# A new order for the instruction list of a convolution followed by a two-layer SiLU network

## The chip, the cores and the metric

The kernel runs on one core of one Trainium2 chip. The core has a matrix engine (TensorE, PE in the profile), a vector engine (VectorE, DVE), a scalar engine (ScalarE, ACT), GpSimd (POOL) and SyncE (SP). Each takes its instructions in the order in which the program gave them, and they wait for one another by semaphores. Matrix products go to eight accumulation banks, from which only VectorE and ScalarE read. Transfers are issued by SyncE or GpSimd. The metric is the device time of one execution in microseconds; lower is better.

## The reference

The input x has 8 sequences of 4096 tokens with 192 channels. A depthwise convolution over the last seven tokens comes first, its weights a softmax over the seven taps for each of eight heads of 24 channels. Its output, 32768 tokens by 192, goes through a network with 2048 hidden units.

```python
x_unf = x_pad[:, idx, :].reshape(B, S, K, H, group)
out = np.einsum('hk,bskhg->bshg', w, x_unf)      # conv, K = 7
...
h = x @ w_in                                     # 192 -> 2048
g = h * (1.0 / (1.0 + np.exp(-h)))               # SiLU
return (g @ w_out).astype(np.float32)            # 2048 -> 192
```

All is float32 on the chip.

## The kernel before, in words

**Blocks.** The tokens are cut into 32 blocks of 1024, two tiles of 512 each. Blocks 0 to 2 are started up by an own order (START); from then on one list (PLAN) is gone through once per pass, b = 3 to 33. Both are strings of tokens; `step` (from L863) turns a token into instructions. A leading "-" means the block before b, "=" two before, "+" the next block. The instructions are pinned: each engine gets them exactly in the order of the tokens. So one string sets the order on all engines at once, and a token that waits on an engine holds up that engine's later tokens. A token is carried out once per block; what was done already is skipped.

**What a pass does.** It makes the hidden values of block b, the output of block b - 1 and the convolved input of block b + 1.

**The conv (GpSimd, ScalarE, SyncE).** `ld.k` loads a third of the input (12 transfers of 64 KB for all), `i.k` turns it (VectorE), `ha.0` fetches the six tokens ahead of the block. `v.ki` is tap i of third k: ScalarE scales the shifted input into one of ten tiles `u` (L499) and GpSimd issues a transfer that adds this tile into `nat` (L500); the six adds of a third go into the same tile, one behind another. `sp.k` (SyncE, L521) copies the finished third to both halves of the 128 rows, into the tile `dup`, and `w.0` to `w.5` (VectorE) make sums and differences of it in the tile `win`.

**The products of h (L630).** Fast matrix multiplication, in 15 products for each of five groups g: `Pr.g` is a matmul with 64 rows and 128 columns over 512 tokens. Each product lies on one half of the rows: r = 0, 1, 2, 4, 5, 6, 11, 14 on the one (only P14.4 is an exception), the others on the other half; two products of different halves run side by side. The groups come in the order 0, 4, 1, 2, 3. The products of a group run in three chains, each chain in one bank, and between two products of a chain another engine reads the running sum:

- P5, copy u5, P2, copy u4, P6, copy u2, P1, copy u0, P0, copy u1, P14, S3. The copies are ScalarE's (L679), into the same ten tiles as the conv's; S is the SiLU (ScalarE, L691).
- P3, sum X2, P9, X4, P7, a5, P4, a1, P8, a0. The sums are VectorE's (L673); each takes one of the copies (X2 takes u2, X4 takes u4 and so on) and gives its tile back.
- P12, b1, P10, b5, and P13 and P11 into two more banks (after X2 and X4).

`L.nk` (L647) are the matmuls of one chunk that is multiplied plainly, three of them with 512 columns and three with two halves of 256.

**The output (L746).** `Di.je` is one slot of the second layer: four matmuls of 128 rows by 32 columns side by side over 512 tokens (128 tokens for i = 5), for j = 0 to 3 and e = 0, 1: 48 slots for a block. They read SiLU values and the differences `t.jk` of them, which VectorE makes (L714) in three rotating tiles. `y`, `x`, `z` (ScalarE, L804 to L812) and `M` (VectorE) gather the output from the banks, `o.i` turns it and `st.i` stores it (SyncE, L843, three transfers each).

**Where things stand.** In PLAN the output of block b - 1 comes first, all 48 D without a break, and then the products of block b. The one exception is at the list's head: P5.0 of block b and P8.3 of block b - 1, one on each half, directly behind the products of the pass before.

```python
nc.tensor.matmul(to[:, cols], raw(g, *LEFT[e][r], e), rhs[:, cols], start=first, ...)   # P
...
for q in range(4):
    nc.tensor.matmul(accs[b][at][SQ * q : SQ * q + SQ, to], lhs[...], rhs[...], ...)    # D
...
z = free.pop(0)                                                       # v: one of ten tiles
pin(nc.scalar.activation(z, src, AF.Copy, scale=tap))
pin(nc.gpsimd.dma_start(out=dst, in_=z, accum_op=ALU.add))
free.append(z)
```

Of the kernel before, what the change touches and what calls it, by code (L numbers as in the profile page):

```python
# [17 lines left out]
def kernel(  # L18
# [62 lines left out]
    PLAN = (  # L81
# [24 lines left out]
    )  # L106
    START = (
# [731 lines left out]
    def store_out(b, i):  # L839
        for q in range((HD if b else P) // SQ):  # L840
# [5 lines left out]
                )  # L846
            )

    plan = [slot.split() for slot in PLAN.split("|")]
    did, later = set(), []  # L850
    closing = f"S3.{QUEUE[-1]}"
    BACK = {"-": 1, "=": 2, "+": -1}
# [263 lines left out]
```

## Time and profile before

| what | value |
|---|---|
| runs | 2363.18, 2363.6, 2364.36 us (median 2363.6) |
| span of the profiled execution, first to last instruction | 2358.8 us |
| busy: PE, DVE, ACT, POOL | 2350.1, 1784.5, 1488.6, 531.0 us |
| transfers: packets' share of the 16 engines | 33.7% (GpSimd's queue), 23.1% (SyncE's) |
| mean granted clock of TensorE | 0.999 |

The profiled execution is reported by its span; the runs' times also hold what lies before the first and after the last instruction, 4.8 us at the median. A matmul is recorded as two parts (float32), 512 columns at some 0.59 us, and the parts overlap: the start of the next part tells more than a duration. Each row of a timeline has the start, the time from the first start to the last end, the engine and line, what is written and read, and a count; in brackets the idle time of the engine before it and what ended it. Rows with "128*32" are the output's D, rows with "64*128" the products. PEld is the loading of weights.

### The profile page before, as it was taken

The numbers are of one execution on the slowest core, as the hardware profiler recorded it, in microseconds if no ns is written. First come the engines' busy times: TensorE is split into PE (matmuls) and PEld (weight loads), VectorE is DVE, ScalarE is ACT, GpSimd is POOL, SyncE is SP. The second block draws the span as 40 slices with busy tenths as digits, with TensorE's granted clock in tenths as the row PEclk, the third lists the DMA queues.
The fourth block names the chain that finished last, engine by engine and source line by source line (L and its number), as shares of the span: only waits on it lengthen the run. The fifth ranks groups of instructions, "written<-read, shape, count | busy, mean of one in ns | idle before, by whom it ended". The sixth has DMA issues, their size and how long they took to land.

```text
span 2358.8 us, 45531 instructions
## 1 busy us (share of the span) xinstructions
PE 2350.1 (100%) x17630; PEld 1053.1 (45%) x17630; DVE 1784.5 (76%) x2373; ACT 1488.6 (63%) x2779; POOL 531.0 (23%) x672
## 2 busy tenths in 40 slices
PE   9999999999999999999999999999999999999998
PEld 4344444444444444444444454444444444444445
DVE  8898767787777787777877777767778777787676
ACT  5346766667656677566676666765667756667643
POOL 4911122211222112222112221122211222211200
PEclk9999999999999999999999999999999999999999
DMA  7234667656566655666556656556655566565511
GB/s 158 51 66 72 107 106 125 105 103 107 98 121 107 106 105 95 119 116 106 106 106 109 119 99 109 105 99 122 107 106 101 101 116 116 106 109 98 96 23 25
DMA packets 523833, 238.81 MB, mean 101 GB/s; under 512 B 431648, under 2 KB 436768, under 8 KB 523616
## 3 DMA queue, kind: packets, MB, share of 16 engines
q0 software_dynamic: 73024, 133.73, 33.7%
q1 hardware_dynamic: 447392, 101.78, 23.1%
q8 instruction: 138, 2.26, 0.4%
q10 hardware_dynamic: 3200, 0.39, 0.1%
q14 instruction: 79, 0.65, 0.1%
HBM read 31.46 MB, written 25.17 MB: 24 GB/s over the span
## 4 chain that ended last, share of the span: by engine, by line
PE 98%; DVE 1%; DMA 0%; ACT 0%; SPq 0%; issue 0%; ACTq 0%
PE ps L746 47%; PE ps L630 42%; PE ps L647 5%; PE ps L767 2%; PE ps L576 2%; PE ps L1015 1%; DVE t L714 0%; DMA dup<-nat 0%; PE ps L423 0%; ACT g L691 0%; DMA nat<-u 0%; SPq L843 0%; DVE g L673 0%; DVE cmb L163 0%; ACT u L163 0%
## 5 line engine op out<-in xcount | busy, mean ns | idle before, releaser
L500 POOL DMA_DIRECT2D nat<-u x504 | 431.9, 957 | 1598.0 <-ACT u L499 643.4
L630 PE MATMUL ps<-win,wr 64*128 64x512 f32 x1550 | 721.5, 598 | 0.0
L746 PE MATMUL ps<-g,wo 128*32 128x512 f32 x2976 | 703.0, 593 | 0.0
L630 PE MATMUL ps<-win,ws 64*128 64x512 f32 x1550 | 638.3, 599 | 0.9 <-ACT u L679 0.9
L746 PE MATMUL ps<-t,wo 128*32 128x512 f32 (+2 forms) x4528 | 547.8, 446 | 0.0
L679 ACT COPY u<-ps 128x512 f32<-128x512 f32 x775 | 442.5, 587 | 136.7 <-PE ps L630 88.6
L746 PE MATMUL ps<-t,wx 128*32 128x512 f32 x2976 | 495.6, 592 | 0.6 <-DVE t L714 0.5
L630 PE MATMUL ps<-dup,wr 64*128 64x512 f32 x868 | 424.1, 597 | 0.0
L691 ACT ACTIVATE g<-g 128x512 f32<-128x512 f32 x465 | 286.2, 633 | 175.5 <-DVE g L673 175.5
L714 DVE TENSOR_TENSOR t<-g,t 128x1024 f32<-128x1024 f32 x248 | 302.0, 1218 | 109.7 <-PE ps L746 107.4
L714 DVE TENSOR_TENSOR t<-g 128x1024 f32<-128x1024 f32 x248 | 302.5, 1220 | 103.9 <-PE ps L746 82.7
L809 ACT COPY yx<-ps 32x512 f32<-32x512 f32 x150 | 86.8, 579 | 421.5 <-PE ps L746 419.4
L673 DVE TENSOR_TENSOR g<-u,ps 128x512 f32<-128x512 f32 x465 | 314.2, 681 | 42.8 <-PE ps L630 32.0
L499 ACT ACTIVATE u<-xt,taps 128x512 f32<-128x512 f32 x504 | 340.0, 717 | 1.1
L630 PEld LDWEIGHTS ps<-win,wr 64*128 64x128 f32 x1550 | 272.1, 186 | 139.5 <-issue 75.6
L630 PE MATMUL ps<-dup,ws 64*128 64x512 f32 x682 | 328.2, 598 | 0.0
L630 PEld LDWEIGHTS ps<-win,ws 64*128 64x128 f32 x1550 | 255.8, 186 | 135.3 <-issue 58.6
L746 PEld LDWEIGHTS ps<-t,wo 128*32 128x32 f32 x4528 | 188.5, 110 | 273.3 <-issue 266.0
L691 ACT ACTIVATE g<-ps 128x512 f32<-128x512 f32 x465 | 267.8, 599 | 36.2 <-PE ps L630 33.6
L673 DVE TENSOR_TENSOR ps<-u,ps 128x512 f32<-128x512 f32 x310 | 215.0, 694 | 64.3 <-PE ps L630 26.7
L746 PE MATMUL ps<-g,wx 128*32 128x512 f32 x1488 | 250.5, 592 | 0.0
L824 DVE TENSOR_TENSOR cmb<-cmb,ps 96x512 f32<-96x512 f32 x150 | 102.2, 681 | 181.7 <-ACT yx L809 180.7
(92 smaller groups left out, 2010.5 us busy)
## 6 DMA issues: line engine op xcount, KB each, us to landing
nat<-u POOLq DMA_DIRECT2D x504, 256.0 KB, 4.0
dup<-nat SPq DMA_DIRECT2D x345, 128.0 KB, 3.0
nat<-in_x_dram SPq DMA_DIRECT2D x382, 64.0 KB, 2.7
out_dram<-osb SPq DMA_DIRECT2D x376, 64.0 KB, 2.0
raw<-in_moe_w_out_dram SPq DMA_DIRECT2D x8, 384.0 KB, 3.5
raw<-in_moe_w_in_dram SPq DMA_DIRECT2D x12, 192.0 KB, 4.4
ws<-wr POOLq DMA_DIRECT2D x8, 192.0 KB, 5.0
raw<-in_moe_w_in_dram SPq DMA_DIRECT2D x6, 128.0 KB, 3.0
```

What stands on the lines that cost most here:

```text
L499: pin(nc.scalar.activation(z, src, AF.Copy, scale=tap))
L500: pin(nc.gpsimd.dma_start(out=dst, in_=z, accum_op=ALU.add))
L576: nc.tensor.matmul(hs[a, n, e], rows(wr[j], e)[:, a, k, :], rows(d, e)[:, n, k, :], start=k == 0, stop=k == NK - 1,)
L630: nc.tensor.matmul(to[:, cols], raw(g, *LEFT[e][r], e), rhs[:, cols], start=first, stop=True, skip_group_check=True,)
L647: nc.tensor.matmul(banks[PLAIN_BANKS[n and 1 + e]][:, cols], rows(wr[j] if own == e else ws[j], e)[:, a, k, :], rows(dups[b], e)[:, SLOT[e ...
L673: pin(nc.vector.tensor_tensor(out_, u, v, op=op))
L679: pin(nc.scalar.copy(us[b, g, o][:, cols], t1[:, cols]))
L691: pin(nc.scalar.activation(h, src, AF.Silu))
L714: pin(nc.vector.tensor_tensor(t[i // 2][:, i % 2, :], u, v, op=ALU.subtract))
L746: nc.tensor.matmul(accs[b][at][SQ * q : SQ * q + SQ, to], lhs[:, e, SQ * k : SQ * k + SQ], rhs[:, e, ts(q, TB // 4) if i == 5 else to], st ...
L809: pin(nc.scalar.copy(to, acc[3 * (name[0] == "x") + k][n:P, :]))
L824: pin(nc.vector.tensor_tensor(out_, u, v, op=ALU.add))
```

## The change

PLAN is written anew, as one sequence of tokens in place of slots with bars (a slot had no other meaning than its tokens in order). It holds the same 300 steps. What differs:

- **P5.0 and -P8.3** stand no longer at the head of the list but in the middle of the output, with 22 D ahead of them in the list and 24 behind.
- **D0.21 and D1.20** lose their "-": they stand at the list's end, directly behind the block's last product, and so are the first D of the output.
- **a1.3, S5.2 and S5.4** get a "-": they move from the products to the head of the next pass.
- **sp.1** moves from the products to the output stage of the next pass; **ha.0, v.10 and v.20** likewise; **o.2 and st.2** move the other way, from two blocks back to one.
- The order of the other D, of the products, and of what the other engines do among them is new. The conv's steps v.25, v.26, v.06, v.15 and v.16 now stand among the products, in this order; before, these were v.16, v.04, v.05, v.06 and the next block's v.20 and v.10. Near the end of the products two of one half and then two of the other follow each other (P12.3, P8.2, then P11.3, P14.3); elsewhere the halves alternate by pairs.
- START gets "-o.2 -st.2 D0.21 D1.20" at its end, and is else the same.

The functions behind the tokens are unchanged. All lines behind the strings move up by five.

```diff
     PLAN = (
-        "+ld.1 P5.0 | -P8.3 -S1.4 -a0.2 -S4.3 | -D0.00 -t.01 -S0.2 | -D1.00 -S1.2 =o.2 v.00 "
-        "| -D2.01 -t.03 -S5.1 =st.2 | -D2.00 -b5.3 | -D1.20 -sp.0 v.21 -S5.3 | -D4.01 u5.0 "
...
-        "u2.1 b1.4 S4.4 | P5.2 | P10.4 X2.1 | P1.1 a1.4 u5.2 | P9.1 b5.4 | P2.2 u0.1 | P8.4 "
-        "X4.1 | P5.3 u4.2 | P7.1 a0.4 | P0.1 +i.1 u5.3 sp.1 | P12.1 a5.1 | P6.2 u1.1 | P3.2 "
...
-        "| P9.3 a5.2 S0.4 | P0.3 -st.0 | P10.2 S1.0 X4.3 | P14.2 u1.3 | P7.3 b5.2 +v.20 "
-        "-st.3 | P4.2 S0.1 | P12.3 a5.3 S3.1 | P14.3 +v.10 a1.2 | P13.3 | P4.3 S5.2 b1.3 | "
-        "P8.2 S2.3 | P11.3 a1.3 S3.3 | P10.3 S5.4 t.00 S3.2"
+        "-S4.3 -D1.11 -sp.0 -S1.4 -D0.11 -S5.1 -D1.01 -D0.01 -a0.2 -D1.00 -D0.10 -t.01 -t.03 "
+        "-D4.01 -D4.00 ha.0 v.10 -t.10 -t.11 -S5.4 -b5.3 -D2.00 v.20 v.21 -S0.2 -t.02 -D3.01 "
+        "-D2.11 -a1.3 -sp.1 -D0.31 -D2.01 -D2.10 v.00 -D3.00 -t.13 -t.12 -D5.01 v.11 v.22 -S1.3 "
+        "-D4.11 -D4.10 -D5.11 -D5.00 -S5.2 -S1.2 v.01 v.02 -D3.10 -D3.11 -S5.3 -t.20 v.23 v.24 "
+        "P5.0 -P8.3 v.12 -D1.30 -t.21 -D2.20 -t.23 -D4.21 -D4.20 -D5.10 -D2.21 -D0.20 -sp.2 "
+        "v.03 v.04 -D5.20 -t.22 -a0.3 -D3.21 -D1.10 -w.0 -S0.3 -t.30 -t.31 -t.32 v.13 -D2.31 "
+        "-D1.31 -t.33 -D5.30 -D0.00 v.05 -w.1 -w.2 -w.3 -w.4 -w.5 -D0.30 -D1.21 -D5.31 -D5.21 "
+        "-x2.1 v.14 -y1.0 -D4.30 -x2.0 u5.0 -D2.30 -y2.0 -z1.0 -D3.20 -M1.0 -D4.31 -x1.0 -x2.3 "
+        "-x2.2 -y0.0 +ld.1 -M2.0 -D3.31 -D3.30 -M3.0 -M4.0 P2.0 +ld.0 u4.0 P3.0 L.02 P5.4 u5.4 "
+        "-x0.0 L.00 P6.0 L.12 -M5.0 u2.0 L.01 X2.0 -M7.0 P2.4 u4.4 SL.0 L.10 L.11 P9.0 SL.1 "
+        "X4.0 SL.2 P1.0 u0.0 P6.4 u2.4 -M6.0 P13.0 S2.0 P5.1 u5.1 -o.3 P3.4 P7.0 P0.0 u1.0 "
+        "+ld.2 P12.0 P11.0 P1.4 X2.4 P9.4 a5.0 P4.0 P13.4 b1.0 v.25 S4.0 X4.4 P10.0 a1.0 b5.0 "
+        "P2.1 u0.4 P0.4 P7.4 -o.1 S2.4 a5.4 P11.4 v.26 P8.0 a0.0 u4.1 u1.4 S1.0 S4.4 P12.4 P6.1 "
+        "b1.4 u2.1 P14.4 P14.0 S3.4 P3.1 X2.1 P4.4 S3.0 a1.4 P5.2 u5.2 P10.4 b5.4 P9.1 P1.1 "
+        "X4.1 u0.1 -o.2 P2.2 v.06 P8.4 a0.4 P5.3 u4.2 P7.1 -st.3 a5.1 P0.1 -o.0 u5.3 u1.1 S5.0 "
...
+        "-st.2 a5.2 P4.2 P13.3 X4.3 P0.3 u1.3 b5.2 a1.2 P7.3 P12.3 S0.1 S0.0 a5.3 b1.3 P8.2 "
+        "+i.1 P11.3 P14.3 S2.3 S3.3 P4.3 P10.3 D0.21 D1.20 t.00 S0.4 -st.0 +i.0"
     )
     START = (
...
-        "P13.3 -o.3 P4.3 S3.2 b1.3 -st.3 +v.10 P8.2 +v.20 a1.3 P10.3 P11.3 S5.2 t.00 S2.3"
+        "P8.2 +v.20 a1.3 P10.3 P11.3 S5.2 t.00 S2.3 -o.2 -st.2 D0.21 D1.20"
     )
...
-    plan = [slot.split() for slot in PLAN.split("|")]
+    plan = [PLAN.split()]
```

99 rows, old and new, of tables (PLAN, START) are left out of this document.

## The prediction

> **What bounds the kernel now.** I read the page first, then the chain of waits in order of time, then short stretches of the timeline of TensorE, ScalarE and GpSimd.
>
> ```profile
> span 2358.8 us, 45531 instructions
> PE 2350.1 (100%) x17630; PEld 1053.1 (45%) x17630; DVE 1784.5 (76%) x2373; ACT 1488.6 (63%) x2779; POOL 531.0 (23%) x672
> 357.48 36.22 PE ps L746 x384
> 398.62 31.22 PE ps L630 x139
> 429.85 36.22 PE ps L746 x384
> ...
> 2243.82 36.22 PE ps L746 x384
> ```
>
> TensorE is never free, so the time is the length of TensorE's own queue. The last four rows are from the chain: one pass of the list is an output stage (L746) and a product stage (L647, L630). From the first to the last of these output stages lie 26 passes, (2243.82 - 357.48) / 26 = 72.55 us each. The first two are 429.85 - 357.48 = 72.37 apart, the usual pass; a few are longer. The median of the runs, 2363.6, is 4.8 above this span; I sum against the span and add 4.8.
>
> "Busy" hides the loss, so I set the necessary work beside it. All rows from here on are from timelines.
>
> ```profile
> 1011.34 0.60 PE L746 MATMUL ps<-g,wx 128*32 128x512 f32 x3
> 1012.20 0.61 PE L746 MATMUL ps<-t,wx 128*32 128x512 f32 x3
> 1053.39 0.59 PE L630 MATMUL ps<-win,ws 64*128 64x512 f32 x1
> 1054.25 0.59 PE L630 MATMUL ps<-win,wr 64*128 64x512 f32 x1
> 1051.08 0.38 PE L647 MATMUL ps<-dup,ws 64*128 64x256 f32 x1
> 1051.30 0.38 PE L647 MATMUL ps<-dup,wr 64*128 64x256 f32 x1
> 1051.57 1.13 PE L630 MATMUL ps<-win,ws 64*128 64x512 f32 x4
> ```
>
> A D token (four matmuls side by side, two parts each) takes 0.86; a pair of products, one on each half of the rows, also 0.86, one part 0.43. A 256-column part takes half, 0.215. A pass has 40 D at 0.86, 8 short D (D5) at 0.215, 39 pairs and 3 short pairs: 36.05 + 34.76 = 70.81. So 72.55 - 70.81 = 1.74 us per pass are lost, all in the product stage and at its two ends.
>
> **Changing between the two kinds of work.** The start order holds the thing that the change adds: D2.11, then P8.3 and P2.0, then D0.31.
>
> ```profile
> 157.53 0.60 PE L746 MATMUL ps<-t,wx 128*32 128x512 f32 x3
> 158.07 1.13 PE L630 MATMUL ps<-win,wr 64*128 64x512 f32 x4
> 159.13 1.06 PE L746 MATMUL ps<-g,wo 128*32 128x512 f32 x8
> 160.01 1.04 PE L746 MATMUL ps<-t,wo 128*32 128x512 f32 x8
> ```
>
> 157.53 is the second part of D2.11, 160.01 the D after next: 2.48 us for 0.43 + 0.86 + 0.86 = 2.15 of work. A pair in the middle of the output costs 0.33 to 0.34 beyond its own 0.86. In the kernel before, P5.0 and P8.3 stand at the end of the products and pay no change of their own. The changed list makes two more changes in each of 30 passes: 30 x 0.34 = **+10.1 us**. Nothing covers this, since both halves stop.
> The Trainium skill, "TensorEngine Tiling (Array Packing)", section Tiling Modes, says that changing the tiling mode drains TensorE, which speaks against this edit; the row above agrees, at 0.34 for both ways. Were there no drain, the sum below would come out 10.1 lower.
>
> **Short waits in the product stage.** The products accumulate in shared banks: a copy or a sum must have read the bank before the next product writes it.
>
> ```profile
> 1060.27 0.59 PE L630 MATMUL ps<-dup,wr 64*128 64x512 f32 x1
> 1060.28 0.69 PE L630 MATMUL ps<-dup,ws 64*128 64x512 f32 x1
> 1061.98 1.14 PE L630 MATMUL ps<-win,wr 64*128 64x512 f32 x4
> 1063.11 0.69 PE L630 MATMUL ps<-dup,ws 64*128 64x512 f32 x1
> 1063.64 0.59 PE L630 MATMUL ps<-dup,ws 64*128 64x512 f32 x1
> 1062.37 0.69 DVE L673 TENSOR_TENSOR u<-u,ps 128x512 f32<-128x512 f32 x1 [1.18 <-ACT g L691]
> 1064.04 0.58 ACT L679 COPY u<-ps 128x512 f32<-128x512 f32 x1 [0.24 <-PE ps L630]
> 1077.48 0.69 PE L630 MATMUL ps<-win,wr 64*128 64x512 f32 x1
> 1078.02 0.59 PE L630 MATMUL ps<-win,wr 64*128 64x512 f32 x1
> ```
>
> A matmul of 0.69 instead of 0.59 started late: its weights had waited too. 1063.11 is P10.4, which waits for b1.4 (the DVE row), which waits for P12.4, one pair earlier: it starts 0.15 late (the last part of the group before it at 1062.53, plus 0.43) and its second part comes after 0.53 instead of 0.43; together 0.25. P7.3 behind X4.3 (1077.48, 1078.02) has the same form and I price it the same. Behind a copy (0.58) instead of a sum (0.69) it is P14.4 at 1060.28, 0.02 + 0.10 = 0.12. With two pairs between, such a product is hardly ever late. P9.0 needs P6.0, copy u2.0 and sum X2.0 in a row: 1051.57 against 1051.30 + 0.215, plus 1.13 instead of 1.02, is 0.17.
>
> I counted these in both lists. Dependents with one pair between fall from 11 (eight behind a sum, three behind a copy) to 8 (four and four). Gone: P12.4/P10.4 0.25, P9.3/P7.3 0.25, P0.4/P14.4 0.12, and P9.0 0.17 (half a pair more between): 0.79. New on the half that ends last: P12.3/P10.3 0.25. Then P8.1 and P8.2: their sums a1 also have one pair; today they are covered because the half that P4 runs on is ahead. In the new list it is less ahead, so I charge one of them at 0.20. P6.0, P5.2 and P14.3 are new waits on the other half at 0.12 each, hidden as long as it stays ahead. Net -0.79 + 0.45 = **-0.34 per pass, -10 us**. Bounds: nothing saved if the other half becomes the last (0), or all that is now lost beside the changes, 1.74 less the 0.34 of the two changes that a pass has already, -1.4.
>
> **The transfers behind the copies.**
>
> ```profile
> 1058.64 0.84 POOL L500 DMA_DIRECT2D nat<-u  x1 [5.41 <-ACT u L499]
> 1063.19 0.85 POOL L500 DMA_DIRECT2D nat<-u  x1 [3.58 <-ACT g L691]
> 1066.58 1.07 ACT L679 COPY u<-ps 128x512 f32<-128x512 f32 x2 [1.10 <-DMA nat<-u]
> nat<-u POOLq DMA_DIRECT2D x504, 256.0 KB, 4.0
>   DMA nat<-u: 28.3, 24
> L499 ACT ACTIVATE u<-xt,taps 128x512 f32<-128x512 f32 x504 | 340.0, 717 | 1.1
> ```
>
> The last three are from the page's DMA issues, from the copies' line (24 waits, 28.3 us) and from the page's groups. A u copy takes one of ten tiles in turn, and a conv step (v) holds its tile until its transfer lands, 4.0 us after issue. Copy u4.2 takes the tile of v.06, seven pairs earlier, and v.06's transfer is issued late (1063.19) because v.05 adds into the same tile and goes first (1058.64). ScalarE stands 1.10, then P6.2 is late; this explains most of the 72.55 - 72.37 = 0.18. In the new list v.05 stands in the output stage, far from v.06; the nearest copies are u2.1 behind v.25 and u4.2 behind v.26. v.25 can run behind u1.0, which is ready some six pairs (5.5 us) ahead of u2.1, against 0.72 + 4.0 + a little; v.26 behind S2.4, some nine pairs ahead of u4.2, with v.25's landing in between. I take **-0.18 per pass, -5.4 us**; bounds 0 (the wait moves to u2.1) and the whole 28.3.
>
> **Edits that I cost at nothing, with their cover.** D0.21 and D1.20 move to the list's end, ahead of the other D: same count, and S3.2, which D1.20 reads, stands eight pairs earlier. a1.3, S5.2 and S5.4 move from the product to the output stage; there VectorE and ScalarE have room:
>
> ```profile
> 1010.40:1046.60 36.20, 36.20 (x385) 12.04 (x384) 23.97 (x26) 17.01 (x31) 11.15 (x13) 1.00 0.70 126
> 1046.60:1082.80 36.20, 36.20 (x172) 20.13 (x168) 30.11 (x47) 30.89 (x59) 4.37 (x6) 1.00 0.52 90
> L714 DVE TENSOR_TENSOR t<-g,t 128x1024 f32<-128x1024 f32 x248 | 302.0, 1218 | 109.7 <-PE ps L746 107.4
> dup<-nat SPq DMA_DIRECT2D x345, 128.0 KB, 3.0
> ```
>
> (columns: stretch, length, busy PE, PEld, DVE, ACT, POOL, clock, DMA; output stage, then products). P8.3 in the middle makes a0.3, S0.3 and t.30 to t.33 later. D5.30, ten D and two short D (9 us) behind P8.3, waits for t.33; behind P8.3 VectorE owes a0.3, w.0 and four t at 1.22 (L714's mean in the row above), with 0.69 (the DVE row above) for each of the others 6.3 us, plus what t.21 to t.22 leave over: by my count about 0.3 us remain, the tightest place. If that cover is gone, each 0.1 costs 3 us. The step sp.1 (four transfers, 3.0 us to landing) moves from the products to the output stage, some 9 us ahead of P5.0, which reads them; ha.0 and sp.0 stand ahead of it on SyncE, and behind them the loads. If it lands late, P5.0 stops all of TensorE in mid output. o.2 and st.2 move from the next pass's output to the products: one transpose on VectorE and three stores on SyncE. The start order only gains these tokens at its end.
>
> **Sum.** 10.1 - 10.2 - 5.4 = -5.5: 2358.8 - 5.5 = 2353.3 in the profile, **2358 us** in the runs.
>
> **Rivals.**
> (1) *The change of mode decides* (slower). The short waits are now partly hidden behind one another, two halves being late in turn; if taking four away only uncovers others, the 10.1 stands alone, or with the transfers' -5.4 half won: 2363.6 + 10.1 - 2.7 = 2371. It decides as soon as stage and transfers give back less than 0.34 per pass. For it: both halves lose about the same now. Against: the late rows that I can name (0.25, 0.25, 0.12, 0.17) all follow a dependency that the new list loosens. 0.27.
> (2) *A new wait in the output stage*, at D5.30 or P5.0, 0.3 per pass: +9, 2367. Against: 26 output stages in the chain are 36.22 long almost without exception, so the present order of the same steps runs without any. 0.14.
> (3) *Most of the lateness goes*: with fewer sums and copies in the product stage only 0.5 of the 1.4 remains besides the changes, -0.9 + 0.34 per pass: about 2347. 0.11.
> (4) *Misplaced halves.* Late in the new list stand P12.3, P8.2 (same half), then P11.3, P14.3 (other half). If matmuls start strictly in the order of the list, one pair's time is lost in 29 passes, 25 us: 2383. The trace speaks against it:
>
> ```profile
> 128.97 1.55 PE L630 MATMUL ps<-win,ws 64*128 64x512 f32 x5
> 130.02 1.02 PE L630 MATMUL ps<-win,wr 64*128 64x512 f32 x2
> ```
>
> The five are P0.2, P9.2 and P1.3; the two are P12.2, which the start order lists before P1.3. P1.3 (last part by 129.93) went first. 0.04. "TensorE: Matmul & The Clock Gate" in the Trainium skill (Part 3, The mechanism) says that matmuls start in strict order without reordering; the trace's 129.93 before 130.02 differs, so I keep the small chance.
>
> **Chances.** The sum holds 0.44, from about 2353 to 2364. A measurement of this kernel can tell 0.2%, 4.7 us. Faster by more: most of the forecast's part and (3), 0.44; within: the rest of the forecast's and the mild ends of (1) and (2), 0.26; slower: 0.30. Eight in ten reach from (3) to just past (1): 2346 to 2375. The forecast's own range is 2352 to 2364.
>
> **What would show it.** The chain's pieces: output stages broken in two by a short L630 piece, together 37.4 (36.22 + 0.86 + 0.34) long; product stages shorter by 0.86 + about 0.5; the pass 72.55 less 0.19. The copies' wait for nat<-u well below 28.3 us. No 0.69 rows at P10.4 and P7.3, one at P10.3. Wrong would be: a gap ahead of D5.30 or P5.0, P14.3 starting 0.86 after its turn, or product stages as long as now.

## The result, and the profile after

The changed kernel takes **2353.2 us** (median of 4 runs, 2352.7 to 2353.8). The kernel before, run beside it, takes 2363.9 (4 runs, 2363.2 to 2364.4). The ratio is 0.9955, with a 95% interval of 0.9941 to 0.9969: faster by 0.45%. The forecast was 2358; its own range was 2352 to 2364, and eight chances in ten lay from 2346 to 2375.

The page of the changed kernel, and its chain of waits in order of time (start, length, what, number of instructions). All line numbers are five lower than before: L741 is the output (D), L625 and L642 are products.

```profile
span 2351.0 us, 45656 instructions
PE 2343.4 (100%) x17630; PEld 1123.6 (48%) x17630; DVE 1802.6 (77%) x2373; ACT 1507.6 (64%) x2779; POOL 528.7 (22%) x672
```

```profile
230.14 1.06 PE ps L625 x4
231.20 17.54 PE ps L741 x192
...
283.56 18.82 PE ps L741 x192
302.38 1.06 PE ps L625 x4
303.44 17.54 PE ps L741 x192
...
2254.83 17.54 PE ps L741 x192
```

The output stage is now broken in two by a short piece of products, 18.82 + 1.06 + 17.54 = 37.42 long; 37.4 was forecast. The pass is 303.44 - 231.20 = 72.24, and over all 28 passes (2254.83 - 231.20) / 28 = 72.27. Before, the usual pass was 72.37 and the mean 72.55. So two things moved: the usual pass became 0.13 shorter, and the passes became equal. An excess of 0.18 per pass over the usual one went down to 0.03.

The profile fell by 7.8 and the runs by 10.7. The profiled execution of the changed kernel took 2352.7 in all, 1.7 more than its span. With the same 1.7, the profiled execution of before took about 2360.5 (an estimate), less than the median of its runs: the 4.8 that the prediction added was 1.7 outside the span and 3.1 because that one execution was a quick one. Executions of before lie between 2359.0 and 2365.8 in all the runs beside the experiments, those of the changed kernel within 1.1 us. So the irregular part of the passes is probably larger in the median run than in the profile that I predicted from; no second profile of before shows it.

The timeline of TensorE in the changed kernel, around the new pair, at D5.30, and at two places among the products of a later pass:

```profile
1022.39 2.75 PE L741 MATMUL ps<-t,wo 128*32 128x512 f32 x33
1025.06 0.69 PE L625 MATMUL ps<-dup,wr 64*128 64x512 f32 x1
...
1025.60 0.59 PE L625 MATMUL ps<-dup,wr 64*128 64x512 f32 x1
...
1026.12 0.63 PE L741 MATMUL ps<-g,wx 128*32 128x512 f32 x3
...
1026.58 0.60 PE L741 MATMUL ps<-g,wx 128*32 128x512 f32 x3
...
1035.17 0.40 PE L741 MATMUL ps<-t,wo 128*32 128x128 f32 x8
...
1207.07 0.59 PE L625 MATMUL ps<-win,ws 64*128 64x512 f32 x1
...
1207.59 0.69 PE L625 MATMUL ps<-win,wr 64*128 64x512 f32 x1
...
1219.95 0.59 PE L625 MATMUL ps<-win,ws 64*128 64x512 f32 x1
...
1220.58 0.69 PE L625 MATMUL ps<-dup,wr 64*128 64x512 f32 x1
...
1221.86 0.59 PE L625 MATMUL ps<-win,wr 64*128 64x512 f32 x1
...
1222.44 0.69 PE L625 MATMUL ps<-dup,ws 64*128 64x512 f32 x1
...
1222.97 0.59 PE L625 MATMUL ps<-dup,ws 64*128 64x512 f32 x1
```

The last part of the D before the pair starts at 1024.54 (the 2.75 from 1022.39 end at 1025.14, less 0.60 for one part) and is worth 0.43. P5.0 starts 0.09 after these 0.43 are over (1025.06), its second part is 0.11 late (1025.60), the next D 0.09 (1026.12) and its second part 0.03: 0.32 for the change both ways, and no wait for the transfers of sp.1. D5.30 (1035.17) starts without a gap. The two rows at 1207 are the product ahead of P7.1 and P7.1 itself, which starts 0.09 after its half is free (1207.07 + 0.43) and takes 0.69. The last rows are P11.3 (1220.58, on a half that was free at 1219.95 + 0.43, so 0.20 late) and P10.3 (1222.44 after 1221.86 + 0.43, 0.15 late, second part another 0.10). How near it was at D5.30 is in VectorE's timeline:

```profile
1033.66 1.22 DVE L709 TENSOR_TENSOR t<-g,t 128x1024 f32<-128x1024 f32 x1
```

This row is t.33. It ends at 1034.88, 0.29 ahead of D5.30.

The copies' line, and then the conv steps' line, idle time of ScalarE until a transfer and how often:

```profile
  DMA nat<-u: 0.3, 1
```

```profile
  DMA nat<-u: 2.9, 11
```

The copies waited 0.3 us in all for a transfer (before: 28.3), the conv steps 2.9.

In the product stage the usual pass now has these late places on the half that ends last, from the timeline of an even pass (late start plus late second part): P10.4 0.10, P9.1 0.06 + 0.10, P7.1 0.09 + 0.10, P10.3 0.15 + 0.10. Together 0.70. That is what is left of the pass above the necessary 70.81 and two times 0.34 for the changes of mode: 72.24 - 70.81 - 0.68 = 0.75. The same sum for the kernel before is 72.37 - 70.81 - 0.34 = 1.22; read in the same way, its late places on that half are P9.0 0.17, P14.4 0.12, P10.4 0.25, P9.1 0.10, P7.1 0.26 and P7.3 0.26, together 1.16.

So of 10.7 us: the changes of mode cost 10; the short waits gave back 0.47 x 30 = 14; the rest, some 7, I put down to the irregular part (0.15 x 30 = 4.5 of it are in the profiles; that most of the 3.1 above belongs to it too is argued, not shown). The experiments ask each of these.

### The profile page after: what moved, and what is told of

It reads as the page before. It is cut to its first block, busy times and chain, and to the rows that moved or that the text cites. A ratio compares the mean times of both kernels' runs of the same rounds, so it can differ in the third digit from the quotient of the medians.

```text
span 2351.0 us, 45656 instructions
## 1 busy us (share of the span) xinstructions
PE 2343.4 (100%) x17630; PEld 1123.6 (48%) x17630; DVE 1802.6 (77%) x2373; ACT 1507.6 (64%) x2779; POOL 528.7 (22%) x672
## 4 chain that ended last, share of the span: by engine, by line
PE 100%; DVE 0%; ACT 0%; issue 0%; ACTq 0%; DVEq 0%
PE ps L741 48%; PE ps L625 44%; PE ps L642 3%; PE ps L762 2%; PE ps L571 2%; PE ps L1010 1%; PE ps L418 0%; DVE cmb L158 0%; ACT u L158 0%; DVE osb L158 0%; DVE xt L460 0%; PE ps L444 0%; ACTq L944 0%; DVE zeros L158 0%; DVE xt L158 0%
## 5 line engine op out<-in xcount | busy, mean ns | idle before, releaser
L625 PE MATMUL ps<-win,wr 64*128 64x512 f32 x1550 | 685.8, 598 | 0.0
L741 PE MATMUL ps<-g,wo 128*32 128x512 f32 x2976 | 681.4, 594 | 0.0
L625 PE MATMUL ps<-win,ws 64*128 64x512 f32 x1550 | 629.5, 596 | 0.0
L674 ACT COPY u<-ps 128x512 f32<-128x512 f32 x775 | 452.3, 584 | 133.3 <-PE ps L625 110.7
L741 PE MATMUL ps<-t,wo 128*32 128x512 f32 (+2 forms) x4528 | 523.6, 446 | 0.0
L741 PE MATMUL ps<-t,wx 128*32 128x512 f32 x2976 | 474.7, 592 | 0.0
L686 ACT ACTIVATE g<-g 128x512 f32<-128x512 f32 x465 | 277.2, 625 | 262.6 <-DVE g L668 262.6
L625 PE MATMUL ps<-dup,wr 64*128 64x512 f32 x868 | 420.2, 598 | 0.0
L625 PEld LDWEIGHTS ps<-win,wr 64*128 64x128 f32 x1550 | 261.6, 187 | 113.4 <-issue 61.8
L625 PEld LDWEIGHTS ps<-win,ws 64*128 64x128 f32 x1550 | 254.6, 187 | 124.2 <-issue 53.5
L625 PE MATMUL ps<-dup,ws 64*128 64x512 f32 x682 | 291.9, 599 | 0.0
L741 PEld LDWEIGHTS ps<-t,wo 128*32 128x32 f32 x4528 | 180.3, 110 | 221.6 <-issue 192.7
L741 PE MATMUL ps<-g,wx 128*32 128x512 f32 x1488 | 251.4, 594 | 0.0
L741 PEld LDWEIGHTS ps<-t,wx 128*32 128x32 f32 x2976 | 121.2, 110 | 241.0 <-issue 240.6
L741 PEld LDWEIGHTS ps<-g,wo 128*32 128x32 f32 x2976 | 167.6, 110 | 135.3 <-issue 125.9
```

What stands on the lines that cost most here:

```text
L674: pin(nc.scalar.copy(us[b, g, o][:, cols], t1[:, cols]))
L686: pin(nc.scalar.activation(h, src, AF.Silu))
```

## Experiments

The theory at the start: the pass is the sum that the prediction made (mode changes up, short waits and transfers down). The rivals: the mode change costs more or less than 0.34, the short waits only cover one another, and the regular passes come from something else than the copies' tiles. The changed kernel was not run again beside the experiments: "more than the changed kernel" is against its 2353.2. The kernel before, run beside each group, differs by up to 1.8 us between groups, so such differences are checked by the length of the usual pass.

### The pair alone, and what the pair at the head had covered

On the kernel before, P5.0, P8.3 and u5.0 are moved behind the fourteenth D. Nothing else.

```diff
-"+ld.1 P5.0 | -P8.3 -S1.4 -a0.2 -S4.3 | -D0.00 ...
+"+ld.1 -S1.4 -a0.2 -S4.3 | -D0.00 ...
-... -D4.01 u5.0 -t.02 ... -D2.11 -a0.3 | -D5.00
+... -D4.01 -t.02 ... -D2.11 | P5.0 | -P8.3 u5.0 -a0.3 | -D5.00
```

> The kernel before with one part of the change alone: P5.0 and P8.3 (and u5.0 behind them) go from the list's head to the middle of the output, behind 14 D. If a change of mode there and back costs 0.34 us and nothing covers it: 30 x 0.34 = 10.2 us more than before, 2374 (2370 to 2378). If the pair's place costs nothing, because P5.0 no longer has to wait at the end of the products: within 3 us of before. Product stages 0.86 shorter, output stages 1.2 longer in the first case.

Measured: 2390.2 (ratio 1.0121, 1.0106 to 1.0136), usual pass 73.32, which is 0.95 more, not 0.34. A miss. The pair itself cost 0.34 as said. The rest is a wait at D2.01, 0.57 in the usual pass (0.66 on average) and 0.02 more at its second part, in the timelines of TensorE and of VectorE of this kernel:

```profile
1021.15 0.60 PE L746 MATMUL ps<-g,wx 128*32 128x512 f32 x3
...
1022.15 0.63 PE L746 MATMUL ps<-t,wx 128*32 128x512 f32 x3 [0.39 <-DVE t L714]
```

```profile
1019.11 1.22 DVE L714 TENSOR_TENSOR t<-g 128x1024 f32<-128x1024 f32 x1
1020.24 0.68 DVE L673 TENSOR_TENSOR g<-u,ps 128x512 f32<-128x512 f32 x1
1020.87 1.23 DVE L714 TENSOR_TENSOR t<-g,t 128x1024 f32<-128x1024 f32 x1
```

D2.01 reads t.01, the last row, which ends at 1022.10; free of it, D2.01 would have started at 1021.15 + 0.43 = 1021.58. VectorE has no gap ahead of t.01. With the pair at the head of the stage, the D had started one pair's time later; that pair was the cover for VectorE's sums. The next kernel is this one with two D that read no t put ahead of D2.01:

```diff
-| -D1.00 -S1.2 =o.2 v.00 | -D2.01 -t.03
+| -D1.00 -S1.2 =o.2 v.00 | -D0.11 | -D1.11 | -D2.01 -t.03
```

> The run with the pair alone moved (2390), with two D that need none of the t (D0.11, D1.11) put ahead of D2.01. Theory of the lost cover (the pair in the middle costs 0.34 for the change of mode; the rest of the 0.95 per pass was D2.01 waiting for t.01, since without the pair at the head the D start one pair's time sooner against VectorE): D2.01 waits for nothing, usual pass 72.37 + 0.34 = 72.71, 2372 to 2376. Rival (VectorE is late by more than that, or the wait goes on to the next D that needs a t): a gap at another D of the first half of the stage, 2380 or more.

Measured: 2376.0 (ratio 1.0059, 1.0044 to 1.0074); the chain's output stages behind the pair:

```profile
1250.04 23.98 PE ps L746 x264
...
1322.76 23.98 PE ps L746 x264
```

The usual pass is 72.71 (1322.76 - 1250.04 = 72.72 in these rows): 72.37 + 0.34, and D2.01 waits for nothing. The time is at the upper end of what was expected. The pair alone costs the change of mode, and the move needs D that can be run without t. The changed list has them: D4.01 is its first D with a t, seventh in the list and ninth on TensorE. (Fourteen passes of this kernel were long at P6.2 and two at D2.11, and its copies waited 40.3 us for transfers; I put it down to this that it stands 13.9 above before rather than 10.)

### Two more changes of mode

On the changed kernel, P2.0 and P3.0 are put ahead of the last two D of the stage.

```diff
-... -M2.0 -D3.31 -D3.30 -M3.0 -M4.0 P2.0 +ld.0 u4.0 P3.0 L.02 ...
+... -M2.0 P2.0 P3.0 -D3.31 -D3.30 -M3.0 -M4.0 +ld.0 u4.0 L.02 ...
```

> The changed kernel with the number of mode changes in mid output doubled: P2.0 and P3.0 go ahead of the last two D. If each way there and back costs 0.34: 10.2 us more than the changed kernel's 2353, less up to 2.4 because P6.0 then has its copy in time: 2361 to 2364. If the mode change is free and the product stage's waits set the time: 2351 to 2354.

Measured: 2363.1 (10 runs; ratio to before 1.0005, 0.9995 to 1.0014). The chain's output stages:

```profile
284.29 18.82 PE ps L741 x192
...
356.86 18.82 PE ps L741 x192
```

The pass is 72.57, 0.33 longer, and the run 9.9 us longer than the changed kernel: one more excursion out of the output costs 0.33 and nothing hides it. The Trainium skill, "TensorEngine Tiling (Array Packing)", section Tiling Modes, says that a change of mode drains TensorE; the 0.33 agrees.

### The halves of the last products

The prediction's fourth rival: in the changed list P12.3 and P8.2, of one half, stand before P11.3 and P14.3 of the other. Here P11.3 is put ahead of P8.2.

```diff
-... a5.3 b1.3 P8.2 +i.1 P11.3 P14.3 S2.3 ...
+... a5.3 b1.3 +i.1 P11.3 P8.2 P14.3 S2.3 ...
```

> The changed kernel with P11.3 listed ahead of P8.2, so that the halves alternate to the end. If TensorE looks past waiting products of the other half, only P11.3's lateness (about 0.3) goes, and P10.3 on the other half, late behind b1.3, still ends last: 0 to 2 us less than 2353. If matmuls start strictly in the list's order, a pair's time of 0.86 comes back in 29 passes: 2328.

Measured: 2353.4 (6 runs; ratio 0.9965, 0.9952 to 0.9977), the pass again 72.24. In the changed kernel P11.3 starts 0.20 late and its second part 0.10; here both are on time. P10.3, on the other half, ends last in both. So the order of the two halves in the list costs the half of P11.3 at most 0.30, which it has to spare, and not a pair's 0.86. "TensorE: Matmul & The Clock Gate" in the Trainium skill (Part 3, The mechanism) has matmuls start in strict order; on the two halves of the rows this kernel's times differ from what that would make, some 25 us.

### One short wait put back at a time

On the changed kernel, P7.3 is put ahead of P13.3, so that one pair stands between P9.3 and P7.3 instead of two.

```diff
-... a5.2 P4.2 P13.3 X4.3 P0.3 u1.3 b5.2 a1.2 P7.3 P12.3 ...
+... a5.2 P4.2 X4.3 P7.3 P0.3 u1.3 b5.2 a1.2 P13.3 P12.3 ...
```

> The changed kernel, with P7.3 ahead of P13.3: between P9.3 and P7.3 stands one pair instead of two, as in the kernel before. Theory of the short waits: P7.3 0.25 late on the half that ends last, pass 72.49, 7 to 8 us more than the changed kernel's 2353: 2359 to 2362. Rival (hidden by the other half's lead or by other late products): 2352 to 2355.

Measured: 2361.2 (10 runs; ratio to before 0.9997, 0.9987 to 1.0006), 8.0 more than the changed kernel; usual pass 72.50, 0.26 more. TensorE's timeline of this kernel:

```profile
1221.54 1.21 PE L625 MATMUL ps<-dup,ws 64*128 64x512 f32 x4
1222.40 0.59 PE L625 MATMUL ps<-win,ws 64*128 64x512 f32 x1
1222.75 0.69 PE L625 MATMUL ps<-win,wr 64*128 64x512 f32 x1
...
1223.28 0.59 PE L625 MATMUL ps<-win,wr 64*128 64x512 f32 x1
```

The four of the first row are P14.2 and P10.2. They end at 1222.75, so the last part of P10.2 starts at 1222.16 and its half is free at 1222.59. The other half goes on at 1222.40 without a gap; P7.3 starts at 1222.75, 0.16 late, takes 0.69 instead of 0.59, and its second part comes after 0.53 instead of 0.43: 0.26. This one swap costs three quarters of what the whole change brought.

The same for P12.4 behind P14.4 (one pair again between P12.4 and P10.4, and between P0.4 and P14.4):

```diff
-... S4.4 P12.4 P6.1 b1.4 u2.1 P14.4 P14.0 ...
+... S4.4 P14.4 P6.1 P12.4 b1.4 u2.1 P14.0 ...
```

> The changed kernel, with P12.4 behind P14.4: between P12.4 and P10.4, and between P0.4 and P14.4, stands one pair instead of two, as in the kernel before. Theory of the short waits: P10.4 0.25 and P14.4 up to 0.12 late, less the 0.10 that P10.4 shows already: pass 72.24 + 0.15 to 0.27, 4 to 9 us more than the changed kernel's 2353: 2357 to 2362. Rival (the late products only cover one another, nothing is won or lost by one of them): 2352 to 2355.

Measured: 2358.2 (10 runs; ratio 0.9982, 0.9973 to 0.9992), 5.0 more than the changed kernel, pass 72.40, 0.16 more: P10.4 0.15 + 0.10 late (0.10 before the swap), P14.4 0.05 + 0.10. The two add 0.30, of which 0.16 came through: P9.1, 0.16 late in the changed kernel, is on time here, since the lateness ahead of it covers its wait for a sum. Both runs fall in the range of the short waits' theory. The rival, that late products only cover one another, holds for a half of one of them.

### The copies' tiles, on the kernel before

The prediction put the irregular passes down to u4.2, which waits for the tile of v.06, which waits behind v.05. Five kernels take v.04 and v.05 away from v.06, each built from the kernel before; (d) is (c) with the stores moved as well.

(a) v.04 into the place after P2.0, v.05 into the place of v.04:

```diff
-P2.0 -x2.3 -w.4 | ... L.11 v.04 u4.4 ... a1.0 +ld.0 v.05 |
+P2.0 -x2.3 -w.4 v.04 | ... L.11 v.05 u4.4 ... a1.0 +ld.0 |
```

> The kernel before with only two conv steps moved: v.04 to P2.0, v.05 to L.11, so that v.05's transfer has landed when v.06's is to be issued. If the wait of copy u4.2 for v.06's transfer is what makes the passes of before irregular: the wait for nat<-u on the copies falls from 28.3 us to under 8, the passes become equal, and 0.18 to 0.28 us per pass go: 2356 to 2359. If the irregular passes come from something else (the loads, SyncE's queue): within 2 us of before, passes as uneven as now.

Measured: 2374.5 (ratio 1.0056, 1.0041 to 1.0071), a miss. P6.2 is on time in all passes, as the mechanism has it. But the usual pass is 72.93: ScalarE, with two conv steps between the first copies, makes P6.0, P9.0 and P1.0 late. ScalarE and TensorE of this kernel:

```profile
1053.58 0.59 ACT L679 COPY u<-ps 128x512 f32<-128x512 f32 x1
1054.06 0.72 ACT L499 ACTIVATE u<-xt,taps 128x512 f32<-128x512 f32 x1
1054.68 0.57 ACT L679 COPY u<-ps 128x512 f32<-128x512 f32 x1
```

```profile
1057.26 1.13 PE L630 MATMUL ps<-win,ws 64*128 64x512 f32 x4 [0.20 <-DVE ps L673]
```

The last row starts with P9.0, 0.55 late on its half (0.07 in the kernel before). Besides, five passes are long because D2.11 is late, by 0.3 to 0.5.

(b) v.04 behind v.26, v.05 behind u2.4:

```diff
--D3.30 -x2.1 v.26 -x2.0 | ... L.11 v.04 u4.4 ... +i.2 u2.4 | ... +ld.0 v.05 |
+-D3.30 -x2.1 v.26 v.04 -x2.0 | ... L.11 u4.4 ... +i.2 u2.4 v.05 | ... +ld.0 |
```

> The kernel before, with the additions v.04 and v.05 issued early: v.04 right behind v.26 at the end of the output stage, v.05 behind the copy u2.4, so that v.06 is no longer held back by v.05 on the queue, and no second conv step stands at the head of the products. Theory of the transfers (the irregular part of the passes, 0.18 each, is the copy u4.2 waiting for the tile of v.06): passes equal to each other, P6.2 no longer late, 5 to 8 us less, 2356 to 2359. Rival (the wait goes to another copy or conv step, as in the run with v.04 at P2.0): 2362 or more, with a new late product named by its row.

Measured: 2362.4 (10 runs; ratio 1.0003, 0.9993 to 1.0012), as the rival had it. P6.2 is on time, the usual pass is the old 72.37, and nothing is won. The copies still waited 12.7 us; one row of ScalarE's timeline, and the product behind it:

```profile
842.51 0.58 ACT L679 COPY u<-ps 128x512 f32<-128x512 f32 x1 [1.60 <-DMA nat<-u]
```

```profile
843.15 0.69 PE L630 MATMUL ps<-dup,ws 64*128 64x512 f32 x1 [0.32 <-ACT u L679]
```

It is u1.4, which takes the tile of v.05, and P14.4 behind it. Four other passes are 0.7 to 1.0 long at D2.11 instead. The timeline of VectorE in one of them:

```profile
941.78 1.21 DVE L714 TENSOR_TENSOR t<-g 128x1024 f32<-128x1024 f32 x1
946.61 1.22 DVE L714 TENSOR_TENSOR t<-g 128x1024 f32<-128x1024 f32 x1 [3.62 <-issue]
```

The row with 3.62 is t.10, and by the code (a pool of three tiles holds the t and the staged output) it takes the tile from which st.2 stores the output of an earlier block. In the kernel before, st.2 stands five D (one of them short) ahead of t.10. There VectorE's timeline names the store, in a usual pass (first row) in which D2.11 is on time; the second row is t.10 in a long pass of the same kernel:

```profile
1015.68 1.22 DVE L714 TENSOR_TENSOR t<-g 128x1024 f32<-128x1024 f32 x1 [0.37 <-DMA out_dram<-osb]
...
1381.47 1.23 DVE L714 TENSOR_TENSOR t<-g 128x1024 f32<-128x1024 f32 x1 [3.57 <-DMA dup<-nat]
```

By the landings in the trace the last of the three stores lands at 1015.37 in the first case, 2.0 after its issue, and at 1381.25 in the second, 4.1 after its issue; each time t.10 starts 0.2 to 0.3 later. D2.11 is then 0.68 late, and this pass is 1.0 long. So there is a second cause of uneven passes, which the prediction had not named, though its own profile holds it once.

(c) v.04 behind v.25 and v.05 behind v.26, both late in the output stage; and (d) the same with o.2 and st.2 moved into the product stage, as in the changed list:

```diff
--D0.10 v.25 | ... v.26 -x2.0 ... L.11 v.04 u4.4 ... +ld.0 v.05 |
+-D0.10 v.25 v.04 | ... v.26 v.05 -x2.0 ... L.11 u4.4 ... +ld.0 |
```

```diff
-| -D1.00 -S1.2 =o.2 v.00 | -D2.01 -t.03 -S5.1 =st.2 | ... P2.2 u0.1 | ... P10.2 S1.0 X4.3
+| -D1.00 -S1.2 v.00 | -D2.01 -t.03 -S5.1 | ... P2.2 u0.1 -o.2 | ... P10.2 -st.2 S1.0 X4.3
```

> The kernel before, with v.04 and v.05 both in the output stage (v.04 behind v.25, v.05 behind v.26), so that in the product stage no addition goes ahead of v.06 and no copy takes the tile of a late addition. In the run with v.05 behind u2.4 the wait went from P6.2 to P14.4 (the copy u1.4, 1.3 in a few passes) and five passes lost 0.4 to 0.9 at D2.11, where t.10 waits for the stores of st.2, whose tile it takes. Theory A (two causes: tiles of late additions, and stores issued at the head of the output stage): P6.2 and P14.4 on time, the passes at D2.11 still long, 2358 to 2361. Theory B (tiles alone): all passes 72.37, 2356 to 2358. Rival (the wait goes on to another copy): 2362 or more.

> The same, and o.2 and st.2 moved from the head of the next output stage into the product stage, where the changed kernel has them. Theory A: nothing irregular is left, all passes 72.37, 0.18 x 30 = 5.4 less than before and 2 to 3 less than the run without the stores moved: 2356 to 2358. Theory B: no difference from the run without the stores moved. Rival (the transpose and the stores hold up a sum or a transfer in the product stage): 2362 or more, with a new late product.

Measured: (c) 2375.7 (ratio 1.0055, 1.0039 to 1.0072), (d) 2382.6 (1.0083, 1.0068 to 1.0098): (c) is a miss, and (d) is what its rival said, with a new late product. (c) has P9.0 and P1.0 late like (a), usual pass 72.91, and two passes with D2.11 late (73.55 and 74.93; in the second P2.1 and P14.4 are late too, and a copy waits 0.71 for a transfer). In (d) the transpose o.2, which I put ahead of X4.1 on VectorE, makes P7.1 0.41 later still, usual pass 73.33. But its passes are equal:

```profile
286.14 36.22 PE ps L746 x384
...
359.47 36.22 PE ps L746 x384
...
2265.99 36.22 PE ps L746 x384
```

359.47 - 286.14 = 73.33, and (2265.99 - 286.14) / 27 = 73.33. With both edits no excess is left; with the additions alone it is. This is a strong sign and not quite a proof, as the pass of (d) is 0.42 longer than that of (c), which by itself leaves transfers more time.

(e) v.01 to v.05 spread over the middle of the output stage, where ScalarE has room:

```diff
-| -D5.10 | ... -D4.10 -t.21 | ... -D0.31 | ... -D2.20 | ... -D3.20 -t.33 | -D2.30 v.02 |
+| -D5.10 v.01 | ... -D4.10 -t.21 v.02 | ... -D0.31 v.03 | ... -D2.20 v.04 | ... -D3.20 -t.33 v.05 | -D2.30 |
```

> The kernel before, with v.01 to v.05 spread over the middle of the output stage (as in the changed list), where ScalarE has room, and nothing added at the end of that stage, where the two runs with v.04 or v.05 there made the first copies late (P9.0, P1.0). Theory (the irregular part of the passes is transfers: a copy that waits for the tile of a late addition): P6.2 on time in all passes, P9.0 and P1.0 as before (0.07 + 0.10), P14.4 as before; usual pass 72.37, with at most some passes long at D2.11 (the stores of st.2): 3 to 6 us less than before's 2363, 2357 to 2360. Rival (on this list the transfers can't be mended without a new late product): 2362 or more, with the late product's row.

Measured: 2372.5 (ratio 1.0041, 1.0026 to 1.0055), as the rival had it. The usual pass is 72.37, P9.0 and P1.0 as before, P6.2 on time, and yet eight passes of 28 are long, by up to 5.4. Copies in one of the longest, on ScalarE:

```profile
1860.97 0.58 ACT L679 COPY u<-ps 128x512 f32<-128x512 f32 x1 [1.37 <-DMA nat<-u]
...
1865.28 1.07 ACT L679 COPY u<-ps 128x512 f32<-128x512 f32 x2 [2.57 <-DMA nat<-u]
```

The four longest passes also have the late D2.11, some 38 us ahead of these copies. By the list these are u1.0, and u0.4 with u4.1 behind it; u1.0 takes the tile of v.15 and u0.4 that of v.16: a wait for transfers again, at other places. What these runs together show: on the list before, none of the four places tried for v.05 gains anything.

### The stores put back

The last is the changed kernel, with o.2 and st.2 at the head of the next output stage, where they were.

```diff
-... -D1.00 -D0.10 -t.01 -t.03 -D4.01 ... u0.1 -o.2 P2.2 ... -st.2 a5.2 ...
+... -D1.00 -D0.10 -t.01 =o.2 -t.03 =st.2 -D4.01 ... u0.1 P2.2 ... a5.2 ...
```

> The changed kernel, with o.2 and st.2 put back to the head of the next output stage (o.2 ahead of t.03, st.2 behind it), as in the kernel before. t.10 takes the tile that these stores read, and in the changed list D2.11 stands only five D behind t.03. Theory A (moving st.2 was not free: it took away a wait): t.10 waits for the landing of the stores and D2.11 starts 0.3 to 1.2 late in every pass, 2362 to 2390. Theory B (the move of o.2 and st.2 is worth nothing, as the prediction has it): 2352 to 2355.

Measured: 2420.7 (ratio 1.0245, 1.0229 to 1.0260), 67 more than the changed kernel. Theory A has the mechanism, but the place named was wrong (D3.01, not D2.11), and the time lies 31 above the top of its range (2362 to 2390). VectorE, SyncE and TensorE in one pass of this kernel:

```profile
1039.52 1.18 DVE L709 TENSOR_TENSOR t<-g,t 128x1024 f32<-128x1024 f32 x1
1043.06 1.22 DVE L709 TENSOR_TENSOR t<-g 128x1024 f32<-128x1024 f32 x1 [2.37 <-DMA xt<-xt]
```

```profile
1039.62 1.51 SPq L838 DMA_DIRECT2D out_dram<-osb  x3
```

```profile
1045.06 0.61 PE L741 MATMUL ps<-t,wx 128*32 128x512 f32 x3
...
1047.33 1.06 PE L741 MATMUL ps<-t,wo 128*32 128x512 f32 x8 [1.66 <-DVE t L709]
```

The stores are issued from 1039.62 to 1041.13, and at a median 2.0 to landing (the page's DMA issues) the last lands at about 1043.1, where t.10 starts (1043.06). By the landings in the trace the last store lands at 1042.94; the transfer that the row names lands at 1043.12, after t.10 has started, so it can't be what t.10 waited for. Behind t.10 on VectorE stands t.02, for which TensorE stands 1.66 ahead of D3.01. In this pass D3.01 starts 1.84 late (1047.33 against 1045.06 + 0.43), over the passes 1.4 to 3.3, 1.8 on average, and the mean pass is 74.25, 2.0 more than in the changed kernel. Some of it is TensorE's clock, which was halved behind the longest waits. The stretch from 451 to 452 us of the same kernel, behind a wait of 2.72 (length, busy PE, PEld, DVE, ACT, POOL, clock, DMA, GB/s):

```profile
451.00:452.00 1.00, 1.00 (x12) 0.28 (x8) 0.00 (x0) 1.00 (x3) 0.28 (x1) 0.50 1.07 168
```

The copies wait 0.3 us in all for a transfer here, as in the changed kernel: their wait went with the conv steps' places, not with the stores. Moving the stores is worth more than anything else in this change, though it shows only because the new order needs t.10 and t.02 early.

## Why the prediction was right, and where a step of it was not

The direction held, and the time lies in the forecast's own range (2352 to 2364), 4.8 below its middle. The gain was nearly twice the forecast's, 10.7 instead of 5.6: the short waits gave back more than their price, and the kernel before was slower in its runs than in the one profile that the sum stands on.

- **Change of mode, +0.34 per pass.** Right: 0.32 at the pair in the changed kernel, 0.34 in the pair alone with cover, 0.33 in the two more changes (9.9 us for 30 passes).
- **Short waits, -0.34 per pass.** The mechanism was right, the size off: -0.47 (1.22 to 0.75). P10.3 was priced at 0.25 and is 0.25. The charge of 0.20 for P8.1 or P8.2 was wrong: neither is late. Without it the step would have said -0.54; it missed that P10.4 keeps 0.10 of its lateness. Two late places that it did not name, P9.1 and P7.1, changed little (0.10 and 0.26 before, 0.16 and 0.19 now). The price of one wait behind a sum, 0.25, was measured at 0.26 by putting one back. In the profile this is 3.9 us below the forecast; less 0.9 by which the transfers gave less and 0.7 that stays unexplained (the start and the end of the run are not in these passes), the profile came out 2.3 lower than predicted. The other 2.6 of the 4.8 is the time outside the span, 2.2 to the median instead of 4.8.
- **Transfers, -0.18 per pass.** The amount was about right in the profile (0.18 to 0.03), but too small for the runs, since the profiled execution of before was some 3 us quicker than the median. The cause named was the larger one, and not the only one: of the 4.7 us by which the 26 passes of that profile exceed the usual pass, seven passes late at P6.2 hold 3.4, one late at D2.11 1.0, and one late at P10.4 0.2. That v.05 stands apart from v.06 does take away the wait at P6.2, in all the runs that did it, but on the old list another wait came in its place. The second cause, the tile that t.10 takes from the stores, has D2.11 late in one pass of before, five of (a), four of (b), two of (c), four of (e), and in none of (d), where the stores are moved. That the step gave about its amount is thus partly luck: the change moved the stores too, which the step had not counted. What each of the two would give alone stays open: the stores alone were not moved in the old list, and of the additions no place was found that left the rest as it was.
- **"Edits that I cost at nothing".** o.2 and st.2 were costed as one transpose and three stores that find room. They do, but the step looked only at what they cost in the new place, not at what waited for them in the old one: 2.0 per pass, if the new order is taken without this move. D1.20's cover is smaller than said: S3.2 stands five pairs ahead of it in the list, not eight, which was enough. The predicted cover at D5.30, "about 0.3 us", was 0.29. No wait at P5.0 for sp.1, as said.
- **The rivals.** The mode change did not decide: stage and transfers gave back twice what it cost. No new wait came into the output stage; the runs show two that would have, at D2.01 (0.57, without D that need no t first) and at D3.01 (1.8 on average, with the stores left where they were). The argument against this rival, output stages "almost without exception" 36.22 long, passed over the one that was not, with D2.11 0.68 late. Most of the lateness did not go: 0.75 of 1.22 is left, so 2347 was not reached. Misplaced halves cost nothing that the time shows.

## What to carry to other kernels

Before moving a piece of work away from a spot, ask what it was hiding there: a pair of products at the head of a stage was the time in which another engine made the next operands. When a transfer's tile makes one engine wait, list everything that takes a tile from that pool, and which transfer frees it, before moving one of them: each wait mended alone here came up again at another taker. And where the passes of a kernel are uneven and its runs spread over several us, the uneven part is worth a term of its own, sized by the runs rather than by one profile.

## What the runs showed of the hardware that was not expected

A small step on ScalarE or VectorE in a tight place passes on by more than half: one conv step of 0.72 among the first copies of a stage made a product 0.48 later, and a transpose of 0.70 ahead of a sum made one 0.41 later, on engines that are busy 63% and 75% of the time in those kernels.

A wait of TensorE can cost more than its length. In the kernel with the stores put back, the granted clock was 0.50 for 3.4 us from 450.33, at the end of a wait of 2.72, and so at four other places, each with a wait of 2.5 or more; in (e) it was 0.50 for 3.4 us in the two longest passes, once from 1867.33, 1.4 after a wait of 1.45 had ended. A matmul part that else starts 0.43 behind the last one then starts 0.85 behind it. A wait of 2.46 in the first of these kernels was not followed by it; what decides is not shown.

And the time of one and the same program varied by 6.7 us over the 25 runs of the kernel before that stand beside one group of experiments (2359.2 to 2365.8), but by 1.1 over the four of the changed one and by 0.7 to 1.2 over ten each of three kernels built from it. That the uneven passes make this spread is argued and not shown by a run of its own; it fits that (d), with equal passes, spread by 0.4 over four runs and (e), with the most uneven of the five, by 7.0 over five.
